# Attention output products in every second slot, and the last tokens' output in parts of 352 and 160 columns

## The chip, the cores and the metric

One NeuronCore of a Trainium2 chip. The metric is the device time of one execution in microseconds (us). Ratios are computed as the mean time of one kernel's fast runs over the mean time of the other's fast runs of the same rounds, with a 95% interval, so they are not quite the ratio of the medians quoted beside them.

## The reference

Linear attention on 8 batches, 8 heads, 576 tokens and head size 64, then a feed-forward layer of 4608 tokens x 512 columns, hidden size 2048, with the activation h + sin(alpha h)^2 / alpha:

```python
q_s = softmax(q, over the head dimension);  k_s = softmax(k, over the tokens)
kv  = einsum('bhsd,bhse->bhde', k_s, v)
x   = einsum('bhsd,bhde->bhse', q_s, kv)          # -> tokens x 512
h   = x @ w_in
g   = h + sin(alpha * h) ** 2 / (alpha + 1e-9)
out = g @ w_out
```

## The kernel before

`b` is a batch of 576 tokens, `t` a stage of 512 tokens, `ni` one of 16 slots in a stage, `ii` one of two head groups of four heads each. `attn_back` is given the slot number less 5, so its `n` of 5 is slot 10. An *evacuation* is the copy that empties a finished product's buffer, here `xp` into `xT`; the *combine* is VectorE's last step of the activation; a DMA *lands* when its completion is signalled.

```python
def q_transpose_dma(b):
    A["qT", b] = att2.tile([128, J, 2, 128], BF16, name="qT")
    nc.sync.dma_start(out=A["qT", b].rearrange("p j ii c -> p (j ii) c"),
                      in_=A["qn", b].rearrange("p j c -> p (j c)"), transpose=True)

XO = ((0, 4), (4, 9))
def attn_out(b, ii, half, pool, eng):                     # pool ps_a has ONE buffer
    j0, j1 = XO[half]
    xp = pool.tile([128, 2, 512], F32, name="xp", tag="a")
    for e in range(2):
        nc.tensor.matmul(xp[:, e, 0:n], kt[:, e, ii], qT[:, j0:j1, ii, e * 64:(e + 1) * 64], ...)
    eng(xT[:, 2 * ii:2 * ii + 2, c0:c0 + n], xp[:, :, 0:n])
# ...
def attn_back(b, n, engs=(DVE_CP, DVE_CP)):
    if n == 0:
        kv_mm(b, 0, ps_a); kv_mm(b, 1, ps_a); kv_norm(b)
    elif 5 <= n < 9:
        attn_out(b, (n - 5) // 2, (n - 5) % 2, ps_a, engs[n % 2])
# ... stage 2: h_slot(2, ni, ...); flush(lag, 2); attn_back(3, ni - 5, (DVE_CP, ACT_CP))
for t in range(3, nT):
    b = t + 1 if t + 1 < B else None
    os = o_stream(t - 1)                                   # output matmuls of the stage before
    for ni in range(nN):
        hp = mm_h(t, ni)                                   # four matmuls
        if b is not None:
            if ni == 4:
                q_transpose_dma(b)
            attn_back(b, ni - 5)
        s = sine(t, ni, hp, "A")                           # ScalarE: sine, square
        combine(t, ni, hp, s)                              # VectorE
        if b is not None and ni == 0:
            exp_q(b); exp_k(b); cast_v(b, [GP, GP]); norm_q(b, [GP])
            if b + 1 < B:
                load_batch(b + 1)
        # ... take some output matmuls
# ... the last 128 tokens, in two parts of 256 columns
for h in range(2):
    cols = slice(h * 256, h * 256 + 256)
    # ... 16 matmuls, a VectorE copy, two stores of 64 rows
```

The softmax here doesn't subtract the row's maximum and nothing guards it: scores larger than these inputs give would overflow.

## Time and profile before

| | before |
|---|---|
| time, median of the first three runs | 296.62 us (296.46 to 296.97) |
| span of the profiled run | 294.8 us |
| TensorE (PE) busy | 279.5 us, 95% |
| from the start of the last matmul to the end of the span | 4.5 us |

PE bounds the kernel; only its stops matter. The lines on which that rests are in the prediction below. A measure is a stage's length: from the end of its first `hp` (issue of the fourth matmul plus 0.216 us) to the same point of the next stage.

### The profile page before, as it was taken

How to read it: one execution, taken by the hardware profiler on the slowest of the kernel's cores; microseconds unless marked ns; L12 is line 12 of the kernel's file. 1: busy time of each engine (PE TensorE's matmuls, PEld its weight loads, DVE VectorE, ACT ScalarE, POOL GpSimd, SP SyncE). 2: the span in 40 equal slices, each digit the busy share in tenths (PEclk: the TensorE clock that was granted, in tenths of full speed). 3: DMA queues.
4: the chain of work that ended last, by engine and by line, in shares of the span. 5: the costliest groups of instructions: out<-in, count | busy, mean ns of one | idle time of the engine just before them, and what ended most of it. 6: DMA issues, size and time to landing. Idle time of an engine off the chain costs nothing.

```text
span 294.8 us, 4250 instructions
## 1 busy us (share of the span) xinstructions
PE 279.5 (95%) x1576; PEld 132.4 (45%) x1576; DVE 185.9 (63%) x270; ACT 228.1 (77%) x320; POOL 84.6 (29%) x73
## 2 busy tenths in 40 slices
PE   2999999999799999999999999999999999999994
PEld 1544445444344444444444444444444444444443
DVE  3758955789638857865687568756875455555421
ACT  4679855999578899879987999799977777777500
POOL 0939590575665536000700061005000000000000
PEclk9999999999999999999999999999999999999999
DMA  7999989955859986108921794112411111111143
GB/s 261 281 191 207 366 234 364 390 189 165 183 85 323 392 282 139 28 21 290 330 50 36 235 337 98 36 39 60 91 38 36 36 36 38 36 36 37 46 99 72
DMA packets 35221, 45.77 MB, mean 155 GB/s; under 512 B 15856, under 2 KB 19712, under 8 KB 35200
## 3 DMA queue, kind: packets, MB, share of 16 engines
q1 hardware_dynamic: 29600, 34.09, 40.6%
q0 software_dynamic: 5408, 11.27, 14.9%
q8 instruction: 12, 0.20, 0.3%
q10 hardware_dynamic: 192, 0.14, 0.2%
q14 instruction: 9, 0.07, 0.1%
HBM read 36.71 MB, written 9.44 MB: 157 GB/s over the span
## 4 chain that ended last, share of the span: by engine, by line
PE 75%; DVE 9%; ACT 5%; POOL 3%; DMA 3%; issue 2%; ACTq 0%; SPq 0%
PE op L235 31%; PE hp L215 30%; PE hp L235 4%; DVE g L231 3%; PE xp L198 3%; PE warm L279 2%; POOL s L225 2%; DVE xT L201 2%; ACT s L221 2%; PE kvp L154 2%; DMA qT<-qn 2%; DMA st_q<-in_q_dram 1%; DVE o L241 1%; ACT xT L201 1%; PE op L468 1%
## 5 line engine op out<-in xcount | busy, mean ns | idle before, releaser
L231 DVE SCALAR_TENSOR_TENSOR g<-s,inva_sb,hp 128x512 bf16<-128x512 f32 x130 | 95.3, 746 | 65.1 <-ACT s L223 52.3
L215 PE MATMUL hp<-xT,win 128*128 128x512 bf16 x520 | 129.7, 379 | 0.3
L235 PE MATMUL op<-wout,g 128*128 128x512 bf16 x496 | 123.8, 379 | 0.0
L221 ACT ACTIVATE s<-hp,alpha_sb 128x512 f32<-128x512 f32 x130 | 87.8, 682 | 27.0 <-PE hp L215 23.0
L215 PEld LDWEIGHTS <-win 128*128 128x128 bf16 x576 | 56.1, 98 | 68.3 <-issue 2.3
L235 PEld LDWEIGHTS <-g 128*128 128x128 bf16 x560 | 54.0, 98 | 61.9 <-issue 1.0
L223 ACT ACTIVATE s<-s 128x512 f32<-128x512 f32 x112 | 70.5, 629 | 3.6
L144 POOL TENSOR_TENSOR qn<-qe,qs 128x2304 bf16<-128x2304 bf16 (+1 forms) x8 | 26.6, 3328 | 85.2 <-DVE qs L143 79.5
L225 POOL TENSOR_TENSOR s<-s 128x512 f32<-128x512 f32 x27 | 28.4, 1058 | 25.9 <-ACT s L221 25.7
L241 DVE COPY o<-op 128x512 f32<-128x512 f32 (+1 forms) x33 | 21.9, 663 | 14.2 <-PE op L235 11.8
L142 DVE TENSOR_REDUCE qs<-qe 128x18 f32<-128x1152 bf16 (+1 forms) x11 | 20.7, 1880 | 13.1 <-ACT qe L114 13.0
L114 ACT ACTIVATE qe<-st_q 128x1152 bf16<-128x1152 f32 x16 | 17.8, 1155 | 2.8 <-DMA st_q<-in_q_dram 2.7
L114 ACT ACTIVATE ke<-st_k 128x1152 bf16<-128x1152 f32 x16 | 17.7, 1150 | 2.5 <-DMA st_k<-in_k_dram 2.5
L128 POOL CAST vb<-st_v 128x1152 bf16<-128x1152 f32 x14 | 16.5, 1210 | 7.9 <-DMA st_v<-in_v_dram 7.9
L201 DVE CAST xT<-xp 128x512 bf16<-128x512 f32 (+1 forms) x22 | 16.5, 753 | 2.8 <-PE xp L198 2.7
L198 PE MATMUL xp<-qT,kbd 128*128 128x256 bf16 (+1 forms) x64 | 12.4, 285 | 4.2 <-ACT xT L201 1.8
L235 PE MATMUL hp<-wout,g 128*128 128x512 bf16 x64 | 15.1, 379 | 0.4 <-DVE g L231 0.3
L198 PEld LDWEIGHTS <-kbd 128*128 128x128 bf16 x64 | 6.0, 97 | 12.9 <-issue 5.7
L201 ACT CAST xT<-xp 128x512 bf16<-128x512 f32 (+1 forms) x10 | 6.3, 638 | 7.0 <-PE xp L198 6.9
L279 PE MATMUL warm<-qe,identb 128*128 128x512 bf16 x19 | 7.5, 562 | 2.8 <-ACT qe L114 2.8
L154 PE MATMUL kvp<-vb,ke 64*128 64x130 bf16 x288 | 9.8, 216 | 0.4 <-ACT qT L183 0.3
L114 ACT ACT_TABLE_LOAD x7 | 9.0, 1283 | 1.3 <-PEq L484 1.2
(51 smaller groups left out, 112.2 us busy)
## 6 DMA issues: line engine op xcount, KB each, us to landing
out_dram<-o SPq DMA_DIRECT2D x70, 128.0 KB, 2.4
st_q<-in_q_dram SPq DMA_DIRECT2D x5, 1152.0 KB, 6.3
st_k<-in_k_dram SPq DMA_DIRECT2D x5, 1152.0 KB, 8.7
st_v<-in_v_dram SPq DMA_DIRECT2D x5, 1152.0 KB, 10.7
st_k<-in_k_dram POOLq DMA_DIRECT2D x2, 1152.0 KB, 10.8
wout<-in_moe_w_out_dram POOLq DMA_DIRECT2D x4, 512.0 KB, 14.4
st_q<-in_q_dram SPq DMA_DIRECT2D x2, 576.0 KB, 4.6
st_k<-in_k_dram SPq DMA_DIRECT2D x2, 576.0 KB, 6.6
```

Source lines behind the costliest of these rows:

```text
L114: nc.scalar.activation(dst[:, :, ii * 128:(ii + 1) * 128].rearrange("p j (x d) -> p x j d", x=2), src[:, ii::2], AX.Exp)
L142: nc.vector.tensor_reduce(part, src, axis=AXL.X, op=ALU.add)
L144: engs[h].tensor_tensor(dst, src, part.unsqueeze(3).to_broadcast([128, J, w, D]), op=ALU.mult)
L198: nc.tensor.matmul(xp[:, e, 0:n], kt[:, e, ii], qT[:, j0:j1, ii, e * 64:(e + 1) * 64], start=True, stop=True)
L201: eng(xT[:, 2 * ii:2 * ii + 2, c0:c0 + n], xp[:, :, 0:n])
L215: nc.tensor.matmul(hp, win[:, ki, ni * 128:(ni + 1) * 128], xT[:, ki, t * MF:(t + 1) * MF], start=(ki == 0), stop=(ki == 3))
L221: nc.scalar.activation(s, hp, AX.Sin, scale=alpha_sb[:, ni:ni + 1])
L223: nc.scalar.activation(s, s, AX.Square)
L225: nc.gpsimd.tensor_tensor(s, s, s, op=ALU.mult)
L231: nc.vector.scalar_tensor_tensor(G[t][:, ni], in0=s, scalar=inva_sb[:, ni:ni + 1], in1=hp, op0=ALU.mult, op1=ALU.add)
L235: nc.tensor.matmul(acc, G[t][:, ni, j * 128:(j + 1) * 128], wout[:, ni, :], start=(ni == 0), stop=(ni == nN - 1))
L241: eng(o[:, cols], acc)
```

## The change

Its intent: the four attention products of a batch stood in four slots running and waited for the one `xp` buffer. They now stand in every second slot, so that VectorE has two slots for each evacuation. The last tokens' output is split unevenly, so that less is left to copy and store after the last matmul. The normalised and the transposed queries are laid out by head group first, which splits one GpSimd multiply, and each copy of PE-made transposes, in two.

```diff
 def norm_q(b, engs):
-    A["qn", b] = qn = att1.tile([128, J, 4 * D], BF16, name="qn")
+    A["qn", b] = qn = att1.tile([128, 2, J, 2 * D], BF16, name="qn")
     # ...                         one multiply over 4 heads -> two over 2 heads each
+    for ii in range(2):
+        engs[ii % len(engs)].tensor_tensor(qn[:, ii]..., qe[:, ii], ..., op=ALU.mult)
 def q_transpose(b, g, pool, eng):
-    eng(qT[:, j0:j1]..., tp[:, 0:m, 0:6])
+    for ii in range(2):
+        eng(qT[:, ii, j0:j1]..., tp[:, 0:m, ii, 0:3])
 def q_transpose_dma(b):
-    nc.sync.dma_start(out=A["qT", b].rearrange("p j ii c -> p (j ii) c"), ...
+    nc.sync.dma_start(out=q_tile(b).rearrange("p ii j c -> p (ii j) c"), ...
-def attn_back(b, n, engs=(DVE_CP, DVE_CP)):
+def attn_back(b, n, engs=(DVE_CP, DVE_CP), xs=(3, 5, 7, 9)):
-    elif 5 <= n < 9:
-        attn_out(b, (n - 5) // 2, (n - 5) % 2, ps_a, engs[n % 2])
+    elif n in xs:
+        m = xs.index(n)
+        attn_out(b, m // 2, m % 2, ps_a, engs[m % 2])
-    attn_back(3, ni - 5, (DVE_CP, ACT_CP))                        # stage 2
+    attn_back(3, ni - 5, (DVE_CP, ACT_CP), (4, 6, 8, 10))
-for h in range(2):                                                # last tokens
-    cols = slice(h * 256, h * 256 + 256)
+for c0, c1 in ((0, 352), (352, 512)):
     # ... (cut: unused helpers, renamed copy engines)
```

So the products stand in slots 8, 10, 12, 14 (stages 3 to 6) instead of 10 to 13, and in stage 2 in 9, 11, 13, 15, there with VectorE and ScalarE exchanged as evacuators.

More of the change, by code (lines that the diff above doesn't have):

```diff
@@ L127, in cast_v @@
         for ii in range(2):
-            engs[ii].tensor_copy(vv[:, 2 * ii:2 * ii + 2, :, 0:D], staged["v", b][:, ii::2])
+            engs[ii](vv[:, 2 * ii:2 * ii + 2, :, 0:D], staged["v", b][:, ii::2])
     def norm_q(b, engs):
-        qe = A["qe", b]
-        A["qn", b] = qn = att1.tile([128, J, 4 * D], BF16, name="qn")
+        qe = A["qe", b].rearrange("p j (ii x d) -> p ii j x d", ii=2, x=2)
+        A["qn", b] = qn = att1.tile([128, 2, J, 2 * D], BF16, name="qn")
         qs = small.tile([128, J, 4], F32, name="qs")
-        n = len(engs)
-        w = 4 // n
-        for h in range(n):
-            cols = slice(h * w * D, (h + 1) * w * D)
-            src = qe[:, :, cols].rearrange("p j (i d) -> p j i d", i=w)
-            dst = qn[:, :, cols].rearrange("p j (i d) -> p j i d", i=w)
-            part = qs[:, :, h * w:(h + 1) * w]
-            nc.vector.tensor_reduce(part, src, axis=AXL.X, op=ALU.add)
-            nc.vector.reciprocal(part, part)
-            engs[h].tensor_tensor(dst, src, part.unsqueeze(3).to_broadcast([128, J, w, D]), op=ALU.mult)
+        if len(engs) == 1:
+            nc.vector.tensor_reduce(qs, A["qe", b].rearrange("p j (i d) -> p j i d", i=4), axis=AXL.X, op=ALU.add)
+            nc.vector.reciprocal(qs, qs)
+        for ii in range(2):
+            part = qs[:, :, 2 * ii:2 * ii + 2]
+            if len(engs) == 2:
+                nc.vector.tensor_reduce(part, qe[:, ii], axis=AXL.X, op=ALU.add)
+                nc.vector.reciprocal(part, part)
+            engs[ii % len(engs)].tensor_tensor(qn[:, ii].rearrange("p j (x d) -> p j x d", x=2), qe[:, ii],
+                                               part.unsqueeze(3).to_broadcast([128, J, 2, D]), op=ALU.mult)
     def kv_mm(b, ii, pool, split=False):
@@ L170, with q_tile @@
     TP = ((0, 6), (6, 9))
+    def q_tile(b):
+        if ("qT", b) not in A:
+            A["qT", b] = att2.tile([128, 2, J, 128], BF16, name="qT")
+        return A["qT", b]
     def q_transpose(b, g, pool, eng):
-        if g == 0:
-            A["qT", b] = att2.tile([128, J, 2, 128], BF16, name="qT")
-        qn, qT = A["qn", b], A["qT", b]
+        qn, qT = A["qn", b], q_tile(b)
         j0, j1 = TP[g]
         m = (j1 - j0) // 3
-        tp = pool.tile([128, 2, 8, 128], BF16, name="tp", tag="a")
+        tp = pool.tile([128, 2, 2, 4, 128], BF16, name="tp", tag="a")
         for j in range(j0, j1):
@@ L181, in q_transpose, with q_transpose_ii @@
             for ii in range(2):
-                nc.tensor.transpose(tp[:, h, 2 * jj + ii], qn[:, j, ii * 128:(ii + 1) * 128], identb)
-        eng(qT[:, j0:j1].rearrange("p (h jj) ii c -> p h (jj ii) c", h=m), tp[:, 0:m, 0:6])
+                nc.tensor.transpose(tp[:, h, ii, jj], qn[:, ii, j], identb)
+        for ii in range(2):
+            eng(qT[:, ii, j0:j1].rearrange("p (h jj) c -> p h jj c", h=m), tp[:, 0:m, ii, 0:3])
+    def q_transpose_ii(b, ii, j0, j1, tp):
+        for j in range(j0, j1):
+            nc.tensor.transpose(tp[:, j - j0], A["qn", b][:, ii, j], identb)
     def q_transpose_dma(b):
-        A["qT", b] = att2.tile([128, J, 2, 128], BF16, name="qT")
-        nc.sync.dma_start(out=A["qT", b].rearrange("p j ii c -> p (j ii) c"),
-                          in_=A["qn", b].rearrange("p j c -> p (j c)"), transpose=True)
+        nc.sync.dma_start(out=q_tile(b).rearrange("p ii j c -> p (ii j) c"),
+                          in_=A["qn", b].rearrange("p ii j c -> p (ii j c)"), transpose=True)
     XO = ((0, 4), (4, 9))
@@ L197, in attn_out @@
         for e in range(2):
-            nc.tensor.matmul(xp[:, e, 0:n], kt[:, e, ii], qT[:, j0:j1, ii, e * 64:(e + 1) * 64],
+            nc.tensor.matmul(xp[:, e, 0:n], kt[:, e, ii], qT[:, ii, j0:j1, e * 64:(e + 1) * 64],
                              start=True, stop=True)
@@ L201, in attn_out, with attn_chunk @@
         eng(xT[:, 2 * ii:2 * ii + 2, c0:c0 + n], xp[:, :, 0:n])
+    def attn_chunk(b, c, j0, j1, xp):
+        ii, e = divmod(c, 2)
+        nc.tensor.matmul(xp, kbd[b % 2][:, e, ii], A["qT", b][:, ii, j0:j1, e * 64:(e + 1) * 64],
+                         start=True, stop=True)
     G = {}
@@ L245, in evac_o @@
                                                          in_=o[64 * hf:64 * hf + 64, cols])
-    ACT_CP, DVE_CP = nc.scalar.copy, nc.vector.tensor_copy
+    ACT_CP, DVE_CP, GP_CP = nc.scalar.copy, nc.vector.tensor_copy, nc.gpsimd.tensor_copy
     V, GP = nc.vector, nc.gpsimd
@@ L354 @@
         exp_k(1)
-        cast_v(1, [GP, GP])
+        cast_v(1, [GP_CP, GP_CP])
         for name, x in (("q", q), ("k", k), ("v", v)):
@@ L380 @@
             flush(lag, 1)
-        cast_v(2, [GP, GP])
+        cast_v(2, [GP_CP, GP_CP])
         flush(lag, 0)
@@ L406 @@
     q_transpose_dma(2)
-    cast_v(3, [GP, GP])
+    cast_v(3, [GP_CP, GP_CP])
     nc.scalar.activation(zero, zero, AX.Sin)
@@ L453 @@
                 exp_k(b)
-                cast_v(b, [GP, GP])
+                cast_v(b, [GP_CP, GP_CP])
                 norm_q(b, [GP])
@@ L463 @@
     take(o_stream(nT - 1), 48)
-    for h in range(2):
-        cols = slice(h * 256, h * 256 + 256)
-        acc = ps_o.tile([128, 256], F32, name="op", tag="o")
+    for c0, c1 in ((0, 352), (352, 512)):
+        acc = ps_o.tile([128, dm], F32, name="op", tag="o")[:, 0:c1 - c0]
         for ni in range(nN):
-            nc.tensor.matmul(acc, G[nT - 1][:, ni, 384:512], wout[:, ni, cols], start=(ni == 0), stop=(ni == nN - 1))
-        evac_o(nT - 1, 3, acc, DVE_CP, cols, (nc.sync, nc.scalar))
+            nc.tensor.matmul(acc, G[nT - 1][:, ni, 384:512], wout[:, ni, c0:c1], start=(ni == 0), stop=(ni == nN - 1))
+        evac_o(nT - 1, 3, acc, DVE_CP, slice(c0, c1), (nc.sync, nc.scalar))
 _INS = ['q', 'k', 'v', 'moe_w_in', 'moe_w_out', 'moe_alpha']
```

## The prediction

> **What bounds the kernel now.** I read the page first: busy shares, then the chain of work that ended last.
>
> ```profile
> PE 279.5 (95%) x1576; PEld 132.4 (45%) x1576; DVE 185.9 (63%) x270; ACT 228.1 (77%) x320; POOL 84.6 (29%) x73
> ...
> PE 75%; DVE 9%; ACT 5%; POOL 3%; DMA 3%; issue 2%; ACTq 0%; SPq 0%
> PE op L235 31%; PE hp L215 30%; PE hp L235 4%; DVE g L231 3%; PE xp L198 3%; PE warm L279 2%; POOL s L225 2%; DVE xT L201 2%; ACT s L221 2%; PE kvp L154 2%; DMA qT<-qn 2%; DMA st_q<-in_q_dram 1%; DVE o L241 1%; ACT xT L201 1%; PE op L468 1%
> ```
>
> The reader is to see that TensorE (PE) carries three quarters of the chain, nearly all of it in the two feed-forward products. The kernel works through nine groups of 512 tokens, which I call stages 0 to 8; a stage has 16 slots, in each of which PE makes one hidden block (`hp`, four matmuls) and some output matmuls (`op`) of the stage before. In stages 2 to 6 the attention of the batch needed next is put between the slots, and only there, and at the start and the end, does PE stop. So I went to the timeline of stage 4 (it starts with `hp` at 130.23 us), where the four attention products (`xp`) now stand in four slots running, 10 to 13.
>
> ```profile
> 152.57 0.75 DVE L231 SCALAR_TENSOR_TENSOR g<-s,inva_sb,hp 128x512 bf16<-128x512 f32 x1
> 152.72 0.43 PE L198 MATMUL xp<-qT,kbd 128*128 128x320 bf16 x2
> ...
> 153.24 0.68 DVE L241 COPY o<-op 128x512 f32<-128x512 f32 x1
> 153.42 1.03 PE L215 MATMUL hp<-xT,win 128*128 128x512 bf16 x4
> ...
> 153.84 0.82 DVE L201 CAST xT<-xp 128x640 bf16<-128x640 f32 x1
> ...
> 154.71 0.38 PE L198 MATMUL xp<-qT,kbd 128*128 128x256 bf16 x2 [0.26 <-DVE xT L201]
> ```
>
> There is one `xp` buffer. The second product is done near 153.1, but VectorE (DVE) is in a combine and then an output copy, and evacuates it only from 153.84 to 154.66; the third product starts at 154.71. PE issued its last `hp` matmul at 153.42 + 3 x 0.216 and was free at 153.42 + 4 x 0.216 = 154.28. The stop is 154.71 - 154.28 = 0.43 us; the bracket's 0.26 is less because a matmul's record runs on past its issue. The timelines of stages 3, 5 and 6 show the same bracket, 0.26, at 124.34, 185.06 and 215.43. This is what the change aims at: 4 x 0.43 = 1.72 us.
>
> **What the Trainium skill says.** "TensorE: Matmul & The Clock Gate", section "Wait — 56ns, not 53.3ns?", gives N / 2.4 GHz + about 2.5 ns from one warm matmul to the next, 215.7 ns at 512 columns. The trace agrees: four `hp` matmuls advance PE by 0.86 us. "PSUM — Partial Sum Buffer", section "Engine vs sequencer instructions", says that ScalarE, VectorE and GpSimdE queues are strict FIFO and that matmuls keep program order. The trace agrees: the evacuation above waits for a combine and a copy that stand before it, and no later matmul passes the waiting `xp`. So a product that is placed earlier than its inputs are ready stops PE altogether. "DMA: Bandwidth & Descriptors", section "Anatomy of one DMA — SWDGE (gpsimd) path", puts some 2.0 us of fixed time on a DMA, mostly completion; the small stores of this trace, issued from other queues than that section treats, land after 2.2 to 2.5 us, so a smaller last store can save little.
>
> **The change part by part.**
>
> *Removed.* The products move from slots 10, 11, 12, 13 to 8, 10, 12, 14 (stages 3 to 6). Two slots last about 2.8 us, and an evacuation with a combine and a copy ahead takes 0.75 + 0.69 + 0.82 = 2.26 us at most, so the wait for the buffer should vanish: -1.72 us.
>
> *Added: the first product is two slots earlier, and its input may not be there.* It needs the transposed queries `qT`, from a DMA that starts when GpSimd has normalised them.
>
> ```profile
> 139.40 4.05 POOL L144 TENSOR_TENSOR qn<-qe,qs 128x2304 bf16<-128x2304 bf16 x1 [24.20 <-DVE qs L143]
> ...
> 143.48 3.25 SPq L187 DMA_TRANSPOSE qT<-qn  x1
> ...
> 147.32 1.03 PE L215 MATMUL hp<-xT,win 128*128 128x512 bf16 x4
> ...
> 148.18 0.81 PE L235 MATMUL op<-wout,g 128*128 128x512 bf16 x3
> ```
>
> 148.18 is the end of slot 8's `hp`, where the first product will now stand. The view of the tile `qT` gives issue to landing as 4.9 us here, so landing at 148.4; it was 4.6, 5.7 and 4.6 in stages 3, 5, 6 (landing at 117.6, 179.6, 208.9). The change also makes the landing later: one GpSimd multiply of 2304 columns (4.05) becomes two of 1152, 2.13 each by the group of that shape, less some 0.04 overlap as in other pairs, so +0.17. From a landing to the first matmul behind it passed 0.13 us (78.49 to 78.62 in the chain). PE arrives 17.95 us after the first `hp` of a stage (130.23 to 148.18): at 178.54 in stage 5, 208.90 in 6; in stage 3 at 117.82. New stops: stage 4, 148.4 + 0.30 - 148.18 = 0.5; stage 5, 179.6 + 0.30 - 178.54 = 1.36; stage 6, 0.3; stage 3, 0.1 (with the shift of the next paragraph). That is 2.25. Stage 5's 5.7 us landing is the oddest of them: I take it half way between stage 4's 4.9 and what was seen, 0.95 instead of 1.36. Sum +1.85.
>
> *Stage 2.* Its four products move from slots 10 to 13 to 9, 11, 13, 15, and the two evacuating engines change places: the last one goes to ScalarE (ACT), behind slot 15's sine. Stage 3's first `hp` reads those columns; the order listing of the changed kernel shows its third matmul waiting on ScalarE, where before it waited on VectorE alone. In the timeline before:
>
> ```profile
> 97.78 0.43 PE L198 MATMUL xp<-qT,kbd 128*128 128x320 bf16 x2
> ...
> 98.05 2.75 PE L215 MATMUL hp<-xT,win 128*128 128x512 bf16 x12
> 98.25 0.82 DVE L201 CAST xT<-xp 128x640 bf16<-128x640 f32 x1 [0.41 <-PE xp L198]
> ...
> 100.37 1.25 ACT L221 ACTIVATE s<-hp,alpha_sb 128x512 f32<-128x512 f32 x2
> ```
>
> The last evacuation was done at 99.07, before that `hp` at 99.78. Laying the new order out with the same durations (sine 0.69, square 0.63, evacuation 0.69 for 640 columns, combine 0.75), three waits on the buffer of together some 1.0 us shrink to some 0.2, PE reaches the end of slot 15's `hp` near 98.7, ACT finishes that sine at 99.9 and the evacuation at 100.6, and `hp` of stage 3 ends near 101.05 instead of 100.64. ACT is later by 0.2. Slot 5 of stage 3 already waits some 0.2 (idle 0.31 before 111.41), and of the 0.4 that much is absorbed. Net +0.2.
>
> *The 352 and 160 columns.* PE work is the same: 16 x 352 + 16 x 160 columns against 32 x 256. What follows the last matmul shrinks: a copy of 0.42 us for 256 columns and 0.68 for 512 makes 0.33 for 160. The store falls from 64 to 40 KB each. -0.1 and perhaps -0.05: -0.15.
>
> *Layout.* Each evacuation of PE-made transposes is split by head group, twice in batch 0 and twice in batch 1. One 1.44 us ACT copy becomes two of some 0.8 that overlap a little; the first may start one transpose earlier. +0.05 for each batch, +0.1, as both sit on the chain. The same multiply in the other layout has the same number of elements; nothing else.
>
> Sum: -1.72 + 1.85 + 0.2 - 0.15 + 0.1 = +0.28, from 296.62 to 296.9.
>
> **The rivals.** *The spread simply works*: the transpose lands earlier than I think, or the loads that run beside it (DMA busy 8 and 9 tenths in the slices around 140 and 174) are over by then. Stages 3 and 6 speak for it, with stops of 0.1 and 0.3. Stages 4 and 5 speak against. Then stops of some 0.6 in all remain: -1.72 + 0.6 - 0.15 + 0.3 = -0.97, so 295.6. *The new wait is worse*: stage 5 keeps 5.7 us and stage 2's last evacuation costs its full 0.4 and more: +1.0 beyond mine, 297.9. *ScalarE or VectorE becomes the bound*: ACT has 1.32 us of work for a slot of 1.3 to 1.5 and VectorE 0.75 to 2.2; with the spread VectorE's crowded slots are thinned, so this has little for it; it would leave the time as it was, near 296.6. *A lower clock after the longer stops*: PE's clock row is 9 throughout with stops of up to a microsecond in it already; I give it nothing.
>
> **Range and chances.** My terms are of some 0.1 to 0.9 us on 296.6, and their signs oppose each other. The least certain are stage 5's landing (0.8 either way) and stage 2 (0.5 either way). The range is 295.6 to 297.9. Two per cent is 5.9 us, more than all stops that the change touches taken together, so it stays within 2% almost surely.
>
> **What would show it.** Right: no waits of `xp` for VectorE's `xT` in stages 3 to 6; instead a stop before the first `xp` of stages 4, 5 and 6, put down to the DMA `qT`, of 0.5, 0.5 to 1.4 and 0.3 us; stage 3's first `hp` broken in two by ScalarE's evacuation; GpSimd's `qn` pairs ending 4.2 us after they start; a last copy of 0.33 us. Wrong: no wait for the DMA at all, with the time under 295.5; or the start, before 17.64 us, longer by over 0.3; or a wait for the `xp` buffer that stays although the products stand two slots apart.

## The result and the profile after

The changed kernel took 297.22 us (median of 4 runs, 296.42 to 297.44) against 296.76 us of the kernel before (4 runs); ratio 1.0011, interval 0.999 to 1.0033. The forecast was 296.9, range 295.6 to 297.9. A change that removes a stop of 0.43 us in each of four stages gained nothing.

The page of the changed kernel, busy shares and chain:

```profile
span 295.5 us, 4265 instructions
...
PE 278.4 (94%) x1576; PEld 131.4 (44%) x1576; DVE 185.9 (63%) x272; ACT 228.5 (77%) x322; POOL 85.8 (29%) x78
...
PE 68%; DMA 14%; DVE 7%; ACT 4%; POOL 3%; issue 2%; SPq 1%; ACTq 0%; DVEq 0%; POOLq 0%
```

The work is the same; what moved is the chain: DMA rose from 3% to 14% of it. Not all of that is the transpose: by line, `qT` rose from 2% to 4%; the rest is the load of `win` at the start (4%), and a load of `st_v` (3%) and stores (2%) that the list has before the stops of stages 4 and 5. The chain's list in time puts a piece "DMA qT<-qn" of 5.17 us straight before the first product of stage 4. The timeline of stage 4 shows it (start, length, engine, operation, and in brackets the idle time and its releaser):

```profile
144.24 3.37 SPq L195 DMA_TRANSPOSE qT<-qn  x1
...
147.91 1.03 PE L229 MATMUL hp<-xT,win 128*128 128x512 bf16 x4
...
149.55 0.38 PE L206 MATMUL xp<-qT,kbd 128*128 128x256 bf16 x2 [0.61 <-DMA qT<-qn]
```

PE was free at 147.91 + 0.864 = 148.77 and starts the product at 149.55: a stop of 0.78 us. The landing took 5.2 us from issue at 144.24. The same reckoning gives 0.11, 1.10 and 0.23 us in stages 3, 5 and 6: in all 2.22 us, where 1.72 us were removed. No product waits for VectorE's evacuation in stages 3 to 6 any more. Stage 5, where the stop is longest, reads differently:

```profile
178.62 1.03 PE L229 MATMUL hp<-xT,win 128*128 128x512 bf16 x4
...
180.58 0.38 PE L206 MATMUL xp<-qT,kbd 128*128 128x256 bf16 x2 [0.94 <-DVE g L245]
```

The profile puts it down to a combine of VectorE. But what the product needs of VectorE, the matrix `kbd`, had been ready since 178.34, and the transpose landed at 180.45, 0.13 us before the product; in stages 4 and 6 the product follows the landing after 0.14 us. So this stop too is the transpose's.

Stage 2's end, in the timeline:

```profile
99.87 0.59 PE L229 MATMUL hp<-xT,win 128*128 128x512 bf16 x2
...
99.91 0.67 ACT L235 ACTIVATE s<-hp,alpha_sb 128x512 f32<-128x512 f32 x1
...
100.48 0.68 ACT L209 CAST xT<-xp 128x640 bf16<-128x640 f32 x1
...
101.22 0.59 PE L229 MATMUL hp<-xT,win 128*128 128x512 bf16 x2 [0.75 <-ACT xT L209]
```

Stage 3's first `hp` is broken in two: its third matmul needs columns that ScalarE evacuates only after slot 15's sine.

The last microseconds, in the timelines, before and after:

```profile
289.32 2.25 ACTq L244 DMA_DIRECT2D out_dram<-o  x2
290.62 0.42 DVE L241 COPY o<-op 128x256 f32<-128x256 f32 x1 [1.32 <-PE op L468]
```

```profile
291.48 1.40 ACTq L258 DMA_DIRECT2D out_dram<-o  x2
292.03 0.32 DVE L255 COPY o<-op 128x160 f32<-128x160 f32 x1 [0.58 <-PE op L483]
```

The copy fell from 0.42 to 0.32 us. But from the last matmul to the end of the span the trace shows 4.49 us before and 3.75 after, a fall of 0.74 us that the copy alone doesn't explain.

The lengths that the matmul and sine records give, for every profiled run (us; "start" is the end of stage 1's first `hp`, "tail" the time from the last matmul to the end of the span). Some traces lack 28 of 1576 matmul records; the points used here were found from ScalarE's sines, all of which are there.

| kernel | start | stage 1 | stages 2+3 | stage 4 | stage 5 | stage 6 | tail | span |
|---|---|---|---|---|---|---|---|---|
| before | 50.61 | 32.97 | 47.51 | 30.36 | 30.36 | 30.36 | 4.49 | 294.8 |
| after | 51.30 | 32.95 | 47.44 | 30.71 | 31.04 | 30.16 | 3.75 | 295.5 |
| e1 spread only | 50.74 | 32.93 | 47.34 | 30.43 | 30.78 | 30.00 | 4.60 | 294.9 |
| e2 tail only | 50.72 | 32.92 | 47.50 | 30.35 | 30.35 | 30.35 | 4.74 | 295.1 |
| e3 layout only | 51.32 | 32.92 | 47.51 | 30.36 | 30.36 | 30.35 | 3.99 | 294.9 |
| e4 late first | 50.75 | 32.93 | 47.34 | 29.94 | 29.94 | 29.94 | 3.89 | 292.9 |
| e5 two transposes | 50.58 | 31.74 | 47.34 | 29.94 | 30.71 | 29.94 | 3.88 | 292.3 |
| e6 stage 2 back | 51.68 | 32.92 | 47.19 | 30.54 | 30.83 | 30.16 | 3.74 | 295.2 |
| e7 late, stage 2 by VectorE | 50.62 | 32.93 | 47.48 | 29.94 | 29.94 | 29.94 | 3.73 | 292.8 |
| e8 late, stage 2 back | 51.82 | 32.92 | 47.09 | 29.94 | 29.94 | 29.94 | 3.76 | 293.6 |
| e9 late, stage 2 back, two transposes | 51.40 | 31.75 | 47.09 | 29.94 | 29.94 | 29.94 | 3.88 | 292.1 |
| e10 loads after | 50.84 | 32.90 | 47.42 | 30.14 | 30.20 | 30.19 | 3.76 | 293.6 |
| e11 before, padded | 51.51 | 32.29 | 47.51 | 30.36 | 30.36 | 30.35 | 3.99 | 294.5 |
| e12 before, padded, tail | 50.61 | 32.30 | 47.51 | 30.35 | 30.35 | 30.35 | 3.75 | 293.4 |

Read the table by columns: where no product waits for a transpose, the stage columns repeat to 0.05 us between kernels that share a part, so they tell causes apart far better than whole times, whose runs scatter by half a microsecond and more. Where one waits, they do not: in stages 4 and 5 the changed kernel and e6 have the same code and differ by 0.17 and 0.21 us, because the transpose's landing varies (5.17 and 5.43 us in the one trace, 5.00 and 5.23 in the other). Stages 7 and 8 up to the last matmul, left out of the table, take 68.13 to 68.17 us in every trace. After against before, the stages give -0.07, +0.35, +0.68 and -0.20, in all +0.76; the tail -0.74; the start +0.69. What the start and the tail have to do with the change is a question for the experiments.

### The profile page after: what moved, and what is told of

It is laid out like the page before. It is cut to its first block, busy times and chain, and to the rows that moved or that the text cites. A ratio compares the mean times of both kernels' runs of the same rounds, so it can differ in the third digit from the quotient of the medians.

```text
span 295.5 us, 4265 instructions
## 1 busy us (share of the span) xinstructions
PE 278.4 (94%) x1576; PEld 131.4 (44%) x1576; DVE 185.9 (63%) x272; ACT 228.5 (77%) x322; POOL 85.8 (29%) x78
## 4 chain that ended last, share of the span: by engine, by line
PE 68%; DMA 14%; DVE 7%; ACT 4%; POOL 3%; issue 2%; SPq 1%; ACTq 0%; DVEq 0%; POOLq 0%
PE hp L229 29%; PE op L249 26%; DMA win<-in_moe_w_in_dram 4%; PE hp L249 4%; DMA qT<-qn 4%; DMA st_v<-in_v_dram 3%; PE xp L206 3%; DVE g L245 2%; DMA out_dram<-o 2%; PE kvp L154 2%; PE hh L229 2%; ACT s L235 1%; DVE qs L141 1%; DMA st_q<-in_q_dram 1%; PE op L483 1%
## 5 line engine op out<-in xcount | busy, mean ns | idle before, releaser
L143 POOL TENSOR_TENSOR qn<-qe,qs 128x1152 bf16<-128x1152 bf16 x13 | 27.4, 2127 | 85.7 <-DVE qs L137 67.5
L239 POOL TENSOR_TENSOR s<-s 128x512 f32<-128x512 f32 x27 | 28.3, 1056 | 25.6 <-ACT s L235 25.4
L255 DVE COPY o<-op 128x512 f32<-128x512 f32 (+2 forms) x33 | 21.9, 663 | 14.1 <-PE op L249 11.8
L136 DVE TENSOR_REDUCE qs<-qe 128x36 f32<-128x2304 bf16 x5 | 12.8, 2553 | 11.3 <-ACT qe L114 11.3
L209 ACT CAST xT<-xp 128x640 bf16<-128x640 f32 (+1 forms) x10 | 6.5, 658 | 7.1 <-PE xp L206 7.0
L154 PEld LDWEIGHTS <-ke 64*128 64x128 bf16 x288 | 8.3, 93 | 4.4 <-issue 2.7
L229 PE MATMUL hh<-xT,win 128*128 128x512 bf16 x40 | 9.4, 379 | 0.9 <-DMA win<-in_moe_w_in_dram 0.9
```

What stands on the lines that cost most here:

```text
L143: engs[ii % len(engs)].tensor_tensor(qn[:, ii].rearrange("p j (x d) -> p j x d", x=2), qe[:, ii], part.unsqueeze(3).to_broadcast([128, J, ...
L154: nc.tensor.matmul(kvp[:, e, ii * 130:(ii + 1) * 130], ke[r, j, ii * 128:(ii + 1) * 128], vt[r, j, ii * 130:(ii + 1) * 130], start=(j == 0 ...
L229: nc.tensor.matmul(hp, win[:, ki, ni * 128:(ni + 1) * 128], xT[:, ki, t * MF:(t + 1) * MF], start=(ki == 0), stop=(ki == 3))
L239: nc.gpsimd.tensor_tensor(s, s, s, op=ALU.mult)
L255: eng(o[:, cols], acc)
```

## The experiments

My theory: the stop for the buffer was exchanged for a stop for the transposed queries, of about the same size; start and tail are largely chance. The rivals: the layout, not the slots, makes the loss; the tail's gain is the work of the split. All twelve kernels gave correct results.

**e1, the slots alone.** The kernel before with the new `attn_back` and the new slots; old layout, 256 and 256 columns.

```diff
-    elif 5 <= n < 9:
+    elif n in xs:                 # (3, 5, 7, 9); stage 2: (4, 6, 8, 10)
```

> The kernel before with only the slots of the four attention products moved (8, 10, 12, 14 in stages 3 to 6; 9, 11, 13, 15 and the exchanged evacuating engines in stage 2); old layout, last tokens 256 and 256. Theory (stops exchanged): the stop for the xp buffer goes (-1.72 us), stops for the transposed queries come, each 0.17 us shorter than in the changed kernel because GpSimd multiplies in one piece: 2.22 - 0.68 = 1.5, and stage 2 costs 0.24; in all about 0.0 us against before, 296.5 to 297.0. Rival 1 (the layout causes the late queries, the slots alone are a gain): no stop for qT over 0.2 us, -1.5 us. Rival 2 (the split multiply hardly matters, the landing itself varies): stops as in the changed kernel, +0.7 us.

Measured: 297.11 us against 296.98, ratio 1.0006 (0.9991 to 1.0021). Stages 4, 5, 6 took 30.43, 30.78 and 30.00 us: a stage without any stop takes 29.94 (e4), so the stops are 0.49, 0.84 and 0.06. That is 0.16 to 0.28 us less than in the changed kernel's trace. Of this, 0.17 us is the second GpSimd multiply: in stage 4 the transpose was issued 12.38 us after the stage's start here, 12.55 in the changed kernel. The rest is the scatter of the landing; against e6's trace the differences are 0.05 to 0.16 us. The slots bring the stops; the layout issues the transpose 0.17 us later.

**e2, the tail alone.** The kernel before with 352 and 160 columns.

```diff
-    for h in range(2):
+    for c0, c1 in ((0, 352), (352, 512)):
```

> The kernel before with only the last tokens' output split 352 and 160. In the two traces the time from the last matmul to the end of the span fell by 0.75 us, of which the copy accounts for 0.14. Theory: only the copy and the smaller store are systematic, -0.15 to -0.3 us, the rest is the chance of one straggling store in the trace before. Rival: the whole 0.75 us belongs to the split (the last stores no longer meet others), so -0.75 us and 3.7 us from last matmul to end again.

Measured: 296.71 against 296.98, ratio 0.9992 (0.9978 to 1.0006): a gain too small to be clear. Its trace was against both theories, though: the tail is 4.74 us, longer than before. So the 0.74 us are not the split's doing. What makes a tail long is told at e11.

**e3, the layout alone.** The changed kernel with the old slots, the old evacuators of stage 2, and 256 and 256 columns.

```diff
-    def attn_back(..., xs=(3, 5, 7, 9)):
+    def attn_back(..., xs=(5, 6, 7, 8)):      # and stage 2, last tokens: as before
```

> The changed kernel with the slots and evacuating engines of the kernel before and 256 and 256 columns, so that the layout by head group alone is left. Theory: the transpose lands 0.17 us later but its first reader stands two slots later, so nothing waits; +0.0 to +0.1 us from the split copies, and the time up to the start of stage 1 (49.75 us before, 50.44 after) is not moved by it but by the weights' landing. Rival: the layout causes the start's +0.69 us: stage 1 starts near 50.4 and the time is +0.7 us.

Measured: 296.41 against 296.98, ratio 0.9983 (0.9966 to 1.0000). The stage columns are those of the kernel before, so the layout costs nothing there. The start was late in the trace (51.32), as the rival said, but the time did not rise; it fell by some 0.5 us, which neither expected. The tail is 3.99 instead of 4.49 us with the very same split, which is the size of that fall: the gain of the tail came with the layout.

**e4, the first product one slot later.** The changed kernel with slots 9, 11, 13, 15 in stages 3 to 6.

```diff
-    def attn_back(..., xs=(3, 5, 7, 9)):
+    def attn_back(..., xs=(4, 6, 8, 10)):
```

> The changed kernel with the products of stages 3 to 6 one slot later (9, 11, 13, 15) and all else kept. Theory: the landing of the transposed queries (18.7 us after a stage's first hp at the latest) is by then mostly past, since one slot more gives PE 1.3 to 1.5 us: the four stops of 0.11, 0.78, 1.10 and 0.23 us go (2.2 us), and the stop for the buffer does not come back: 295.0 us. Rival: the last evacuation, in slot 15, comes too late for the next stage's first hp and a new stop of 0.3 us or more per stage comes there: 296.2 us or more.

Measured: 294.68 against 296.98, ratio 0.9923 (0.9908 to 0.9939). All stops of the products in stages 3 to 6 are gone; stages 4, 5 and 6 take 29.94 us each, 0.42 us less than before. That is the whole gain the change was after. The timeline of stage 4:

```profile
148.76 1.03 PE L229 MATMUL hp<-xT,win 128*128 128x512 bf16 x4
149.62 0.38 PE L206 MATMUL xp<-qT,kbd 128*128 128x256 bf16 x2
149.84 0.59 PE L249 MATMUL op<-wout,g 128*128 128x512 bf16 x2
```

The product follows its `hp` after 0.86 us, four matmuls' time, with nothing between. The rival, that the last evacuation would come too late for the next stage, is refuted by the same column.

**e5, two transposes.** The changed kernel, slots kept, with the transposing DMA issued in halves.

```diff
-        nc.sync.dma_start(out=q_tile(b)..., in_=A["qn", b]..., transpose=True)
+        for ii in range(2):
+            nc.sync.dma_start(out=q_tile(b)[:, ii], in_=A["qn", b][:, ii]..., transpose=True)
```

> The changed kernel, all slots kept, but the transposing DMA of each batch issued in two halves by head group, the first as soon as the first GpSimd multiply is done (2.1 us earlier). The first product reads only the first half. Theory (the stop is the arrival of qT and nothing else): the first half lands by 146.7 in stage 4, before PE comes at 148.8; the stops of 0.78, 1.10 and 0.23 us go, stages 4 to 6 take 29.95 us as in the version one slot later, and the time is 294.7 to 295.2 us. Rival: two DMAs share their engines and each has its fixed time, or the first slot is waited for because VectorE's kbd is not ready (0.94 us in stage 5 was put down to VectorE): stops of 0.3 us and more stay, 295.8 us or more.

Measured: 294.71 against 296.92, ratio 0.9921 (0.9901 to 0.9941). Stages 4 and 6 lost their stops (29.94), so these were the arrival of `qT`. Stage 5 kept one, 30.71 - 29.94 = 0.77 us: its halves, issued at 170.1 and 172.2 us, took 7.2 and 5.9 us to land, where those of stages 3 and 6 took 3.2. So the rival had a point in stage 5: something else than the issue sets the landing there (e10 points to the loads; halves without loads beside them were not tried). Stage 1 fell from 32.95 to 31.74 us, which I had not expected: batch 2's first product waits for its transpose too; with its half landed at 76.05 it started at 77.36, without a stop, instead of 78.62 us in the kernel before.

**e6, stage 2 put back.** The changed kernel with slots 10 to 13 and the old evacuators in stage 2.

```diff
-        attn_back(3, ni - 5, (DVE_CP, ACT_CP), (4, 6, 8, 10))
+        attn_back(3, ni - 5, (ACT_CP, DVE_CP), (5, 6, 7, 8))
```

> The changed kernel with stage 2 alone put back (slots 10 to 13, evacuating engines as before). Theory: stage 3's first hp is no longer broken in two by ScalarE's evacuation (a stop of 0.9 us there), but PE gets three shorter stops for the xp buffer again; stages 2 and 3 together shorten by the 0.24 us they lost: 47.5 us instead of 47.73, the time 0.2 to 0.3 us under the changed kernel's. Rival: stage 2's spread is a gain that the break only hides: no change or +0.2 us.

Measured: 296.62 against 296.92, ratio 0.9983 (0.9964 to 1.0002). Stages 2 and 3 took 47.19 us instead of 47.44, 0.25 us less, as expected (the expected absolute figures count stage 2 from another point and are 0.3 us higher). The spread of stage 2 is a loss.

**e7, stage 2's last evacuation on VectorE.** e4 with the evacuators of stage 2 exchanged.

```diff
-        attn_back(3, ni - 5, (DVE_CP, ACT_CP), (4, 6, 8, 10))
+        attn_back(3, ni - 5, (ACT_CP, DVE_CP), (4, 6, 8, 10))
```

> The version one slot later (9, 11, 13, 15 everywhere), with the evacuating engines of stage 2 exchanged, so that the last one is VectorE's and no longer stands behind ScalarE's sine of slot 15. Theory: the break of 0.9 us in stage 3's first hp shrinks to 0.3 us or none, ScalarE's order then decides, 0.2 to 0.5 us under the version one slot later: 294.2 to 294.5 us. Rival: VectorE is behind too (its combines wait for GpSimd's squares) and the stop stays: 294.7 us.

Measured: 294.77 us, ratio 0.9926 (0.9906 to 0.9945): no better than e4. The rival was right; the timeline shows the stop still there, now put down to VectorE:

```profile
98.94 0.59 PE L229 MATMUL hp<-xT,win 128*128 128x512 bf16 x2
99.80 0.82 DVE L209 CAST xT<-xp 128x640 bf16<-128x640 f32 x1
100.67 0.38 PE L229 MATMUL hp<-xT,win 128*128 128x512 bf16 x1 [1.14 <-DVE xT L209]
```

Not the engine, but the slot is at fault: a product in slot 15 can't be evacuated by either engine before the next `hp` comes.

**e8, both put right.** e4 with stage 2 as before.

> The version one slot later in stages 3 to 6, with stage 2 as in the kernel before (slots 10 to 13). Theory: both losses of the change are taken back and both gains kept: 0.24 us under the version one slot later, 294.4 us, stages 2 and 3 together 47.4 us (47.81 before less the 0.43 us stop). Rival: as for the stage 2 put back alone, 294.7 us.

Measured: 294.37 against 296.92, ratio 0.9907 (0.9888 to 0.9927). Stages 2 and 3 take 47.09 us, 0.25 less than in e4, as expected; the difference between e8 and e4 in whole times lies within their intervals.

**e9, e8 with two transposes.** The diff is e8's and e5's together.

> Slots 9, 11, 13, 15 in stages 3 to 6, stage 2 as before, 352 and 160 columns, and the transposing DMA of each batch in two halves by head group. Theory: stages 4 to 6 take 29.94 us as in the version without the halves; in addition the first product of batch 2, which stops PE for the whole transpose after stage 1's outputs, gets its half 1.2 us earlier (78.6 to 77.4 in the version with halves): 1.2 us under the version one slot later with stage 2 put back (294.37), so 293.2 us. Rival: the gain of 1.2 us is taken back in stage 2 by later evacuations or by GpSimd, 294.2 us or more.

Measured: 293.90 against 296.87 us, ratio 0.9897 (0.9881 to 0.9913): the fastest version, 1.0% under the kernel before. Stage 1 gave its 1.17 us and nothing was taken back in any stage; the whole time is 0.7 us above the forecast 293.2 and below the rival's 294.2, and the intervals of e8 and e9 are too wide to say more.

**e10, the loads after the transpose.** The changed kernel with the next batch's three loads of 1.15 MB issued behind the transposing DMA.

```diff
                 norm_q(b, [GP])
-                if b + 1 < B:
-                    load_batch(b + 1)
 # ... in slot 4
                     q_transpose_dma(b)
+                    if b + 1 < B:
+                        load_batch(b + 1)
```

> The changed kernel with the loads of the next batch issued after the transposing DMA instead of before it, nothing else. The stops for qT were large only in stages 4 and 5, where loads were in flight beside the transpose (landing 5.2 and 5.4 us against 4.6 in stages 3 and 6). Theory (the loads stretch the landing): all transposes land in 4.6 us, stages 4 and 5 take 30.1 to 30.2 us as stage 6 does, instead of 30.71 and 31.04: 1.4 us under the changed kernel, 295.8 us. Rival 1 (the issue time and the fixed time set it, the loads don't): stages 4 and 5 stay. Rival 2: the loads are then too late for the next stage's exponentials and a new stop comes, no gain.

Measured: 295.84 against 296.87, ratio 0.9966 (0.9948 to 0.9984). All four transposes landed in 4.6 us, and stages 4, 5, 6 took 30.14, 30.20 and 30.19 us. So of the 0.78 and 1.10 us stops in the changed kernel's trace, 0.57 and 0.84 us went with the loads; some 0.2 us a stage remain because the slot is too early even for an undisturbed landing. Moving the loads also moved an instruction fetch out of stage 4's transpose (145.3 us in the changed kernel, 151.5 here), a rival that e11 makes plain. It does not hold here: in stage 5 a 16 KB fetch at 174.2 us still lies in the transpose, which landed in 4.60 us, and in e5 no fetch lies in stage 4's halves, which still took 5.8 and 4.7 us. The DMA packets agree: the transpose's 2304 packets start within 2.9 us where no loads run in stages 3 to 6, and within 2.9 to 3.9 us beside them. So loads often stretch a transpose, but not always by the same amount: in e7 stage 4's landed in 4.59 us beside them.

**e11, fourteen useless instructions.** The traces' packets show what makes a tail long. In the kernel before, e1 and e2 an 8 KB packet of instruction fetch starts 1.90 to 1.94 us after the last matmul, amid the last stores, and the last store lands at 3.45, 3.58 and 3.71 us; of the completion signals of the last stores, all but the last two have come 0.46 to 0.99 us earlier. In the kernels of the new layout, which have more instructions, the fetch starts by 0.7 us and no gap is over 0.13 us. The edit adds instructions to the kernel before while its engines wait for the first loads:

```diff
+    pads = [singles.tile([128, 1], F32, name=f"pad{n}") for n in range(3)]
+    for _ in range(4):
+        nc.vector.memset(pads[0], 0.0)
+        nc.scalar.copy(pads[1], zero)
+    for _ in range(6):
+        nc.gpsimd.memset(pads[2], 0.0)
```

> The kernel before with 14 tiny instructions of no use added in the first microseconds, while the engines wait for the first loads (four each on VectorE and ScalarE, six on GpSimd), nothing else. In the traces of all three kernels with the old layout (before, spread only, tail only) an 8 KB instruction fetch starts 1.9 us after the last matmul, amid the last stores, and one store lands 0.5 to 1.0 us after the others; with the new layout, which has 15 instructions more, the fetch starts by 0.7 us and no store is late. Theory (the count of instructions ahead places the fetch): with the padding the fetch comes earlier, the last landing is at 2.97 us after the last matmul and the end at 3.95 instead of 4.5: -0.5 us, 296.4 us. Rival (the straggler comes by chance or with the layout's data): the fetch stays at 1.9 us or the store is late all the same, no change, 296.9 us.

Measured: 296.00 against 297.17 us, ratio 0.9958 (0.9941 to 0.9975). The DMA view from 291.5 to 294 us, first the kernel before, then e11 (queue, kind: packets, MB, share of 16 engines in the window):

```profile
q1 hardware_dynamic: 80, 0.07, 11.0%
q10 hardware_dynamic: 80, 0.07, 10.4%
q14 instruction: 1, 0.01, 1.6%
```

```profile
q1 hardware_dynamic: 80, 0.07, 11.9%
q10 hardware_dynamic: 80, 0.07, 10.5%
```

The fetch among the stores is gone, the last landing is at 2.97 us and the tail is 3.99 instead of 4.49, as expected. The time fell by twice that, because stage 1 shortened too, from 32.97 to 32.29 us. There batch 2's transpose lands in 4.7 instead of 5.4 us, and in the kernel before a fetch at 77.3 us falls into its last microsecond, which in e11 has moved to 67.0. The chain of the kernel before and that of e11:

```profile
73.13 5.36 DMA qT<-qn
```

```profile
74.03 4.69 DMA qT<-qn
```

That a fetch delays a DMA in flight is shown for the place of the fetch: it was moved, and the delay went, at two places in e11 and again in e12. It is not shown for any fetch. In the ten traces whose stage 1 has an undivided transpose and a fetch 1.16 to 1.24 us before its landing, the landing comes 1.14 to 1.18 us after the transpose's last packet has started; in e11 and e12 it comes after 0.53 and 0.51 us, and in every other undivided transpose of these traces after 0.47 to 0.60 us, also where a fetch ran earlier in it. So it was the end of the transfer that the fetch held up, and only a fetch that stood there did so; by what mechanism is not shown.

**e12, the padded kernel with 352 and 160.** The diffs of e11 and e2 together.

> The padded kernel before with 352 and 160 columns for the last tokens as well. Theory: the smaller last copy and store give 0.27 us once no fetch hides it: last landing 2.71 us after the last matmul, 0.75 us under the kernel before, 296.1 us. Rival: the split has no gain of its own, the same as the padded kernel with 256 and 256.

Measured: 295.28 against 297.17, ratio 0.9938 (0.9921 to 0.9955); last landing at 2.71 us, the tail 3.75 us, 0.24 less than e11's. The split's own gain, of which e2 showed nothing in its trace, is there once no fetch is amid the stores.

## Why the prediction was right

Point by point, by its own terms.

- *Removed, -1.72 us.* Right: e4 against before gives 0.42 us in each of stages 4, 5 and 6, and no wait for the buffer is left.
- *New stops, +1.85 us.* The mechanism was right in every stage; the size was short in the changed kernel's trace. Measured: 0.11, 0.78, 1.10 and 0.23, in all 2.22 us. The mis-sized terms are stage 4 (0.5 forecast; the landing took 5.2 us where 4.9 had been seen before) and stage 5 (0.95 after halving the excess of its landing; 1.10 came). But landings vary: the same stages in e6's trace stop for 0.10, 0.60, 0.89 and 0.22, in all 1.81 us, so the forecast lies between two traces of the same code. Each stop was to be put down to `qT`; stage 5's was put down to VectorE. The halving supposed a landing of 5.3 us in stage 5 and was near: the ten other traces with an undivided transpose and the loads in place show 5.16 to 5.43, so 5.65 was in part an accident of one trace. Stage 6's landing was read as 208.9 from a rounded view; it was 208.82, which makes its stop 0.22. That even 5.3 is more than 4.6 has a cause, the loads beside it (e10).
- *Stage 2, +0.2 us.* Right: e6 against after, and e8 against e4, give 0.25 us each. The laid-out order had the evacuation end at 100.6 (101.16 came; this stretch of the run began 0.7 us late).
- *The split, -0.15 us.* Right in the copy (0.42 to 0.32 us), short in the store: the last landing moved from 2.96 and 2.97 (e3, e11) to 2.71 us (e12, after), in all about -0.26.
- *Split copies, +0.1 us.* The chain shows +0.06 in batch 1 (1.51 us for the pair against 1.45). Batch 0's is hidden: slot 8 of stage 0 waits for the input weights, which landed at 24.4 us in one trace and 25.1 in the other.
- *Not foreseen:* -0.48 us of tail, because the changed program's length moved an instruction fetch out of the last stores (e3, e11). With every other term as measured, 296.62 + 0.54 - 0.48 = 296.7 would have been the sum; two errors of some 0.4 and 0.5 us with opposite signs cancelled, and that was luck. The whole times can't judge terms of this size: the interval of the ratio reaches from -0.3 to +1.0 us.
- *The start, +0.69 us in the profiled run:* it varied from 50.58 to 51.82 us over the traces, and the record shows by what. In every trace the start comes a fixed time after the landing of the sixth load of `win`, for which slot 8 of stage 0 waits: 26.18 to 26.19 us in the old layout, with or without padding, and 26.24 us in the new one. So 0.06 us of the 0.69 belong to the layout, the same 0.06 as above, and the rest is that landing, which lay at 24.3 to 25.6 us. What moves it stays open, but the whole times speak against the layout: over its nine kernels, the change of the time less that of the span after the start is +0.07 us on average (-0.34 to +0.39). The sign of error that the prediction named, the start before 17.64 us, did not come: that point was at 17.27.
- *The rivals:* "the spread simply works" failed for stages 4 and 5 as argued; an engine becoming the bound did not happen, nor a lower clock (1.000 in both profiled runs).
- *A reading that was wrong:* PE stops not only in stages 2 to 6, at the start and at the end. In the kernel before it also stops at the end of stage 1, 1.22 us before the product at 78.62, for batch 2's transpose. The change did not touch this stop; e5, e9 and e11 gained there.

## What to carry to other kernels

Moving work earlier to give one wait room can put it in front of its input: before moving a consumer, write the arrival time of every input beside the new slot, and take the arrival under the transfers that will be in flight there. One slot later kept the gain of the spread and lost the stops (e4), and splitting the producer by consumer opened more (e9, 1.0%). Below half a per cent, compare kernels by stage lengths from their traces, from more than one where a stage waits for a DMA, and remember that a few added instructions alone moved this kernel by 0.4% (e11).

## What the Trainium skill lacked or had wrong

- "DMA: Bandwidth & Descriptors", section "DMA Transpose (X-bar)", gives no time for one transpose within on-chip memory, and the only time found in the skill is for one of 128 x 128: 128 x 2304 bf16 (590 KB) took 4.6 us from issue to landing with no loads beside it, half of it 3.2 us (e5, stages 3 and 6).
- The same page, "Rules for kernel authors", says that a transpose next to ordinary DMAs needs nothing. No run here speaks against that for correctness; in time it can cost: 4.6 to 5.7 us beside 1.15 MB loads (stages 4 and 5), and up to 7.2 us for a half (e5), against 4.6 in e10, where the loads were moved away.
- No page gives a size for what an instruction fetch costs a DMA beside it: with the fetch moved away, the last landing came 0.48 us earlier and one transpose took 4.7 instead of 5.4 us (e11).
- "TensorE: Matmul & The Clock Gate", section "Wait — 56ns, not 53.3ns?", has measured values for few widths; its formula holds for the odd ones too: 149 ns between starts at 352 columns and 69 ns at 160, where N / 2.4 GHz + 2.5 ns gives 149 and 69.
